# Softmax attention beside a dilated window on one core: the first sixteen score blocks under a bound from the first 512 keys

## The chip, the core and the metric

The kernel runs on one core of one Trainium2 chip. A core has five engines with queues of their own: TensorE (PE, matrix products; its weight loads are shown as PEld), VectorE (DVE), ScalarE (ACT, the exponentials), GpSimd (POOL) and SyncE (SP), which here issues nearly all transfers. Each engine works through its instructions in the order in which they were compiled, and waits where an operand is not there yet. The metric is the device time of one execution in microseconds (us); lower is better.

## The reference, cut to what matters

```python
# x: 2048 x 512; H = 32 heads of Dh = 16
def _A_ref(x, wqkv, wo):                     # full attention
    q, k, v = heads(x @ wqkv)
    scores = einsum("bhqd,bhkd->bhqk", q, k) * Dh ** -0.5
    p = softmax(scores)                      # 2048 keys for every query
    return concat(einsum("bhqk,bhkd->bhqd", p, v)) @ wo

def _B_ref(x, wqkv, wo):                     # 8 keys per query: s, s-2, ..., s-14
    q, k, v = heads(x @ wqkv)
    logits = einsum("bhsd,bhswd->bhsw", q, gather(k)) * Dh ** -0.5   # masked below 0
    return concat(einsum("bhsw,bhswd->bhsd", softmax(logits), gather(v))) @ wo

g = sigmoid((x * gate_w).sum(-1))
return g * _A_ref(x, A_wqkv, A_wo) + (1 - g) * _B_ref(x, B_wqkv, B_wo)
```

The bulk of the arithmetic is branch A: 32 heads x 2048 queries x 2048 keys exponentials.

## The kernel before, in words

**Branch A.** A *block* is one head, one tile of 128 keys and one chunk of 512 queries: a 128x512 square of transposed scores. There are 32 x 16 x 4 = 2048 blocks. Four heads form a group `i` (8 groups), and a *period* is one group with one query chunk `c_`, 64 blocks; there are 32 periods, chunks innermost. For each block TensorE multiplies a K tile (`ktg`, a strip of 32 rows per head) with Q (`qtg`), an exponential is taken, and TensorE multiplies the result `pT` into an accumulator bank with V (`vp_all`, with a 17th column that gathers the denominator). A row more in Q and K subtracts, inside the score product, a bound on the score: the sum over the head's 16 dimensions of |q| times the largest |k| of that dimension. Softmax does not depend on what is subtracted, as long as it is the same for all keys of a query.

Most exponentials are ScalarE's: the score products write into two rings in PSUM, `rA` (three blocks) and `rB` (two), and ScalarE takes one set of three or two in one instruction (`ex` in `new_set`, tiles `pT`). Some blocks go another way: "d" blocks are done by VectorE in four instructions (`p1` to `p4`, tiles `dg` and `pd`), "g" blocks by VectorE and GpSimd in one and six (`g1` to `g4`, tiles `gt`); g blocks come only when branch B is through. Their scores stand in one of three shared banks (`bank`).

**The start.** `load_x` brings x transposed in four strips of 512 rows (`xT`), `load_w0` three small pieces of the weights for the first four heads (`w`), all in SP's queue. `warm` issues 16 products on constants. Then K of the first four heads is projected strip by strip (`kp`), VectorE takes the largest |k| of each strip (`km`), ScalarE copies the strip to `ktg[0]` (`kc`); `selk_f` joins the four maxima, and `q_direct` projects Q for chunk 0, takes |q| (`absq`), multiplies it with `selk` and adds the bound to Q (`qe`). Only then can a score product be issued. `v_proj` projects V for eight key tiles at a time, in two halves. Later groups' K and Q come from `k_pack` and `q_pack`, packed for 128 columns and brought into place by transfers.

**Branch B** works on 16 tiles of 128 positions (`b_tile`): TensorE projects, the K and V rows go to memory and come back shifted for the eight neighbours (`sh`, four loads of four neighbours), and GpSimd multiplies and sums: `logits_half` twice, then softmax, then `av_half` twice. TensorE transposes the result `obb` into `obt`.

**The end.** `po1` to `po3` divide and transpose a period's accumulator into `oat`; the output projection adds `obt` times `bwo` and `oat` times `woP` and writes `out`. Three kinds (`mode`): plain, "fa" (all but the last group first, the rest added by VectorE) and "ring".

**What sets the order.** None of it is written in order. Each piece is an `Op` with engine, assumed duration, dependencies, buffers and a due time; `Scheduler.run` plays them through against these numbers, and the instructions are issued in the order that comes out. `Feeder` makes the attention blocks as it goes. The constants at the head (`CFG`, `OVER`, `HOLD`, `GSTEP`, ...) steer the choice. In places where TensorE would pause, `fill` adds products of zeros (`zeros`, shown as `ones_t,z`). All instructions are recorded in one helper, so the profile has line L299 for nearly everything; tiles tell them apart.

Of the kernel before, what the change touches and what calls it, by code (L numbers as in the profile page):

```python
# [18 lines left out]
    b_start=30.0,  # L19
    b_space=43.0,  # L20
    t0=18.0,
    t1=860.0,
    d_rem=1,
    d_min=14,
    d_end=10,
    fa2=-30.0,
# [70 lines left out]
OVER = 20.0  # L97
HOLD = 3.5
SPAN, STREAM = 3.3, 2.5
WAVE, SWITCH, JOIN = 0.222, 0.10, 0.05  # L100
GSTEP = 1.95
# [147 lines left out]
def kernel(  # L249
# [89 lines left out]
    periods = [(c_, i) for i in range(NG) for c_ in range(NC)]  # L339
# [22 lines left out]
    selk = const.tile([128, 128], BF16, name="selk")  # L362
    mask32 = const.tile([128, 32], BF16, name="mask32")
# [11 lines left out]

    def init_dve():
        V.memset(ones_t[:], 1.0)
# [10 lines left out]
        V.memset(z32[:], 0.0)  # L388
        V.memset(gw[:], 0.0)

# [3 lines left out]
    def init_pool2():  # L394
        G.memset(vp_all[:, 0, :, :], VS)
        G.memset(vp_all[:, 1:NT, 0:8, DH:DH + 1], VS)
# [21 lines left out]
    o_init_d = op("dve", 2.5, init_dve, -9.0)  # L418
    o_cr = [op("dve", 1.6, const_rows((1,), (0,)), -8.0, deps=[o_init_d])]
    o_cr.append(op("dve", 0.8, const_rows((), (1,)), 24.0, deps=[o_init_d], rel=20.0))  # L420
    o_cr += [op("dve", 1.6, const_rows((b,), (b,)), 70.0 + 20 * b, deps=[o_init_d], rel=60.0) for b in (2, 3)]
    o_id = op("pool", 1.2, init_pool, -9.0)
    o_init_p = op("pool", 1.5, init_pool2, -8.0, deps=[o_id])
    o_init_p3 = op("pool", 6.0, init_pool3, -7.0, deps=[o_init_p])

# [32 lines left out]
    o_x = [op("sp", 0.5, load_x(0), -9.0, lat=5.0)]  # L458
    o_w0k = op("sp", 0.5, load_w0(1), -8.9, lat=6.0, alloc=[tw0])
    o_x.append(op("sp", 0.5, load_x(1), -8.8, lat=6.5))  # L460
    o_w0q = op("sp", 0.5, load_w0(0), -8.75, lat=7.0, use=[tw0])
    o_x.append(op("sp", 0.5, load_x(2), -8.7, lat=8.0))
    o_x.append(op("sp", 0.5, load_x(3), -8.6, lat=9.5))
    o_w0v = op("sp", 0.5, load_w0(2), -8.55, lat=9.5, use=[tw0])
# [5 lines left out]

    def warm():
# [4 lines left out]
    o_warm = op("pe", 2.0, warm, -9.0, deps=[o_init_d], alloc=[wtok])  # L476

    o_xt = [[o] for o in o_x]

    kt_tok = {i: tok(f"kt{i % 4}", 1) for i in range(NG)}  # L480
# [9 lines left out]
    for sc in range(NC):  # L490
        st = {}
        tk = bank()

        def kp(sc=sc, st=st, tk=tk):
            st["p"] = bank_tile(tk)
            for c in range(DC):
                mm_w0(st["p"], c, 1, xT[:, c, sc * QW:(sc + 1) * QW], c == 0, c == DC - 1)
# [7 lines left out]
        a = op("pe", 0.9, kp, -2.0 + sc, deps=[o_w0k] + o_xt[sc], alloc=[tk], use=[tw0])  # L505
        km0_ops.append(op("dve", 0.7, km, -1.0 + sc, deps=[a, o_init_d], use=[tk]))
        o_kr[0, sc] = op("act", 0.65, kc, -1.0 + sc, deps=[a, o_init_d], use=[tk, kt_tok[0]] if sc else [tk],
                         alloc=[] if sc else [kt_tok[0]])
# [5 lines left out]

    def q_direct(c_, dl):
# [3 lines left out]
        def qp():  # L519
            st["p"] = bank_tile(tk_q)  # L520
            for c in range(DC):
                mm_w0(st["p"], c, 0, xT[:, c, c_ * QW:(c_ + 1) * QW], c == 0, c == DC - 1)

        def qc():
            V.tensor_scalar(out=qtg[0][:, c_, :], in0=st["p"][:], scalar1=rowc[:, 2:3], scalar2=rowc[:, 3:4],
                            op0=ALU.mult, op1=ALU.add)
            st["a"] = work.tile([128, QW], BF16, name="absq", tag="absq", bufs=1)
            V.tensor_scalar(out=st["a"][:].bitcast(U16), in0=qtg[0][:, c_, :].bitcast(U16), scalar1=32767,
# [6 lines left out]
        def qe():  # L535
            V.tensor_tensor(out=qtg[0][:, c_, :], in0=qtg[0][:, c_, :], in1=st["b"][:], op=ALU.add)
        a = op("pe", 0.9, qp, dl, deps=[o_w0q] + o_xt[c_], alloc=[tk_q], use=[tw0])
        a = op("dve", 1.1, qc, dl + 0.9, deps=[a] + o_cr[:1], use=[tk_q] + ([qt_tok[0]] if c_ else []),
               alloc=[ta_q] + ([] if c_ else [qt_tok[0]]))
        a = op("pe", 0.25, qb, dl + 2.8, deps=[a, o_selk], alloc=[tk_b], use=[ta_q])  # L540
        o_qr[0, c_] = [op("dve", 0.7, qe, dl + 3.0, deps=[a], use=[tk_b, qt_tok[0]])]

    NDQ = 2
    for c_ in range(NDQ):
        q_direct(c_, -0.5 if c_ == 0 else 24.0)
# [3 lines left out]
    def k_pack(cc):  # L549
# [3 lines left out]
        for sc in range(NC):  # L553
            dl = base - 95.0 + 9.0 * sc if cc else 40.0 + 1.5 * sc
# [40 lines left out]
        o = op("sp", 0.6 * 4 * len(gs), sct, dl + 10 if cc else 48.0, deps=evs + (o_cr if cc else o_cr[:1]),  # L595
# [5 lines left out]
    def q_pack(cc):  # L601
# [5 lines left out]
        for c in range(NC):  # L607
            dl = base - 48.0 + 6.0 * c if cc else 46.0 + 1.5 * c
# [39 lines left out]
        def sct():  # L648
            for g in range(2):
                c0 = 0 if cc or g else NDQ  # L650
                qt = qtg[(2 * cc + g) % 4]
# [709 lines left out]
```

## Time and profile before

| | |
|---|---|
| median of three runs | 870.23 us (869.83 to 870.89) |
| the profiled execution's own time | 873.02 us |
| its span, first to last instruction | 871.1 us |
| ScalarE busy | 842.1 us, 97% |
| TensorE busy | 793.5 us, 91% |
| VectorE busy | 756.2 us, 87% |
| GpSimd busy | 713.5 us, 82% |
| 16 DMA engines, share by the largest queue | 19.5% |
| blocks on ScalarE, VectorE, GpSimd | 1818, 216, 14 |

Busy time counts an engine once where its instructions overlap, so the mean of one instruction times the count is more than the busy time. "a <- b" behind an idle time names what ended it. The timeline's columns are start, duration, engine, line, operation, out<-in, shape and count. Of a wait the profile names the releaser that came last.

### The profile page before, as it was taken

What the parts mean: (1) busy time and instruction counts of PE and PEld (TensorE: products, weight loads), DVE (VectorE), ACT (ScalarE), POOL (GpSimd) and SP (SyncE); (2) the same over time, 40 slices, a digit from 0 to 9 for tenths busy, and PEclk for the clock granted to TensorE, in tenths of its full rate; (3) what the DMA queues carried; (4) which work ended last, traced back from release to release, by engine and by line L of the source; (5) the groups of instructions that cost most, each with busy time, mean ns of one, the idle gap of its engine ahead of it and who ended that gap; (6) DMA issues with size and microseconds to landing.
All of it is one profiled execution on the core that took longest, in us unless ns stands there. A gap on an engine that the chain in (4) does not pass through costs nothing.

```text
span 871.1 us, 18136 instructions
## 1 busy us (share of the span) xinstructions
PE 793.5 (91%) x7076; PEld 253.5 (29%) x7076; DVE 756.2 (87%) x1228; ACT 842.1 (97%) x751; POOL 713.5 (82%) x737
## 2 busy tenths in 40 slices
PE   6998999998899998999989999998989888899997
PEld 3223333232223332222222333222222222222232
DVE  5989898989999889998999898989889999887665
ACT  2999999999999999999999999999999999999996
POOL 2268989989997999799969997999699964886772
PEclk9999999999999999999999999999999999999999
DMA  9513202223111112221202020401321000000001
GB/s 235 178 19 119 69 26 71 51 55 130 49 61 50 61 50 60 75 78 59 86 26 85 25 86 26 109 26 38 108 76 49 25 2 1 1 2 8 20 26 49
DMA packets 54781, 51.55 MB, mean 59 GB/s; under 512 B 13628, under 2 KB 51172, under 8 KB 54696
## 3 DMA queue, kind: packets, MB, share of 16 engines
q1 hardware_dynamic: 54408, 50.14, 19.5%
q8 instruction: 55, 0.90, 0.4%
q14 instruction: 30, 0.25, 0.1%
q10 hardware_dynamic: 288, 0.26, 0.1%
HBM read 38.04 MB, written 6.33 MB: 51 GB/s over the span
## 4 chain that ended last, share of the span: by engine, by line
ACT 59%; issue 19%; PE 12%; POOL 7%; DVE 1%; SPq 1%; DMA 1%; ACTq 0%; POOLq 0%; DVEq 0%
ACT pT L299 58%; PE bank L299 8%; POOL prod L299 5%; PE ring L299 4%; SPq L299 1%; DMA w<-in_A_wqkv_dram 1%; ACT lg L299 1%; DVE dg L299 0%; POOL lg L299 0%; DMA sh<-kv_scr 0%; POOL ob L299 0%; POOL obb L299 0%; POOL ott L299 0%; DVE accT L299 0%; DVE pd L299 0%
## 5 line engine op out<-in xcount | busy, mean ns | idle before, releaser
L299 ACT ACTIVATE pT<-ring 128x1536 bf16<-128x1536 f32 x727 | 834.1, 1271 | 9.8 <-PE ring L299 6.6
L299 PE MATMUL ring<-qt,kt 32*128 32x512 bf16 x1818 | 290.2, 384 | 53.1 <-ACT pT L299 50.5
L299 DVE SCALAR_TENSOR_TENSOR dg<-bank,dg 128x512 bf16<-128x512 uint16 x432 | 297.1, 688 | 13.3
L299 PE MATMUL bank<-pT,vp_all 128*17 128x512 bf16 (+1 forms) x1818 | 290.6, 384 | 12.8 <-ACT pT L299 9.9
L299 POOL TENSOR_TENSOR prod<-prod 128x512 f32<-128x512 f32 (+1 forms) x208 | 240.4, 1169 | 6.3
L299 DVE TENSOR_SCALAR dg<-bank 128x512 bf16<-128x512 uint16 x216 | 146.8, 679 | 37.2 <-PE bank L299 29.4
L299 PEld LDWEIGHTS <-kt 32*128 32x128 bf16 x2048 | 88.8, 91 | 290.1 <-issue 286.8
L299 POOL TENSOR_TENSOR prod<-sh,qb 128x512 f32<-128x512 bf16 x128 | 143.7, 1154 | 33.7 <-DVE pd L299 32.6
L299 DVE TENSOR_TENSOR pd<-bank,dg 128x512 uint16<-128x512 f32 x216 | 148.9, 689 | 7.6 <-PE bank L299 0.3
L299 PEld LDWEIGHTS <-vp_all 128*17 128x17 bf16 (+1 forms) x2048 | 92.4, 88 | 215.9 <-issue 194.4
L299 PE MATMUL bank<-ones_t,z 128*32 128x512 bf16 x458 | 148.7, 384 | 0.0
L299 POOL TENSOR_TENSOR prod<-sh,lg 128x512 f32<-128x512 bf16 x128 | 137.5, 1106 | 2.1
L299 PE MATMUL bank<-qt,kt 32*128 32x512 bf16 x230 | 88.1, 386 | 0.2
L299 PE MATMUL bank<-pd,vp_all 128*17 128x512 bf16 x216 | 76.9, 385 | 0.1
L299 PE MATMUL bank<-bw,xT 128*32 128x512 bf16 x768 | 68.5, 383 | 0.0
L299 POOL TENSOR_SCALAR gt<-gt 128x512 f32<-128x512 uint16 (+2 forms) x42 | 38.1, 908 | 20.9 <-DVE gt L299 17.9
L299 POOL TENSOR_TENSOR gt<-gt 128x512 f32<-128x512 f32 x42 | 50.0, 1191 | 3.4
L299 PEld LDWEIGHTS <-z 128*32 128x32 bf16 x458 | 37.2, 95 | 40.9 <-issue 27.1
L299 PE MATMUL bank<-xT,wst 128*32 128x512 bf16 x512 | 44.9, 383 | 0.0
L299 PEld LDWEIGHTS <-xT 128*32 128x32 bf16 (+1 forms) x1088 | 32.6, 97 | 26.4 <-issue 19.4
L299 POOL TENSOR_TENSOR rr<-rr,omg 128x32 f32<-128x32 f32 x16 | 3.8, 238 | 33.8 <-DVE rr L299 25.9
L299 DVE STREAM_TRANSPOSE accT<-bank 128x512 f32<-128x512 f32 x32 | 22.7, 709 | 6.1 <-PE bank L299 6.0
(87 smaller groups left out, 418.6 us busy)
## 6 DMA issues: line engine op xcount, KB each, us to landing
sh<-kv_scr SPq DMA_DIRECT2D x64, 512.0 KB
kv_scr<-kvs SPq DMA_DIRECT2D x16, 256.0 KB
kt<-kpk SPq DMA_DIRECT2D x28, 64.0 KB
qt<-qpk SPq DMA_DIRECT2D x28, 64.0 KB
out_dram<-osb SPq DMA_DIRECT2D x14, 128.0 KB
wst<-in_A_wqkv_dram SPq DMA_DIRECT2D x3, 512.0 KB
bw<-in_B_wqkv_dram SPq DMA_DIRECT2D x1, 1536.0 KB
bwo<-in_B_wo_dram SPq DMA_DIRECT2D x1, 512.0 KB
```

What stands on the lines that cost most here:

```text
L299: return chain_on(key, f(*a, **k))
```

## The change

The first 16 blocks (group 0, chunk 0, key tiles 0 to 3, four heads) are bounded by the maximum of the first key strip alone. Their Q is kept apart without a bound (`qf`); a second product of `kneg` (minus the strip's maxima) with `absq` subtracts the bound inside the score product's bank. Their products with V go to an accumulator of their own (`acc_tok["f"]`). When the other strips are there, the two bounds' difference gives a factor per head and query: `rs` forms it with two products (`selb`, `sele`), ScalarE takes the exponential of half of it (`rf`), and VectorE multiplies the accumulator with it twice (`rx`); `po1` adds it to period 0's accumulator, which begins with key tile 4.

Around it: two pieces of the first weights are issued by ScalarE, not SP; the products that stood on `selq` at the start are 13 products of zeros issued at once, and `fill` may add such while they run; K strips 1 and 2 are copied by VectorE; the projections of K, of Q (chunk 1) and of V are cut into smaller pieces; Q's transfers are issued head group by head group; GpSimd handles two neighbours in one instruction; the last eight periods run with the two last groups side by side for each chunk, so the output projection of chunk 2 is plain too; due times and assumed durations differ.

In the compiled order ScalarE has 363 sets of three, 364 of two and 2 of one (364, 363 and none before), VectorE 211 blocks, GpSimd 18. Products of zeros go from 458 to 431, those at the start included. GpSimd has 192 instructions fewer in branch B.

```diff
 CFG = dict(
-    b_start=30.0,
-    b_space=43.0,
-    t0=18.0,
-    t1=860.0,
+    b_start=28.0,
+    b_space=40.0,
+    t0=9.0,
+    t1=848.0,
...
-OVER = 20.0
-HOLD = 3.5
+OVER = 15.0
+HOLD = 1.5
+DQ_DL = 0.6
...
-GSTEP = 1.95
+GSTEP = 2.1
...
-    periods = [(c_, i) for i in range(NG) for c_ in range(NC)]
+    periods = ([(c_, i) for i in range(NG - 2) for c_ in range(NC)] +
+               [(c_, i) for c_ in range(NC) for i in (NG - 2, NG - 1)])
...
-                SP.dma_start(out=w0[:, :, part, :], in_=a_w3[:, :, part * D:part * D + 80])
+                (SP if part == 2 else A).dma_start(out=w0[:, :, part, :], in_=a_w3[:, :, part * D:part * D + 80])
...
+    def zero_w():
+        mm(st_w["t"][0:32, :], z32[:], ones_t[:], True, True, tile_position=(0, 0))
+
     def warm():
-        t_ = bank_tile(wtok)
-        for _ in range(4):
-            mm_ct(t_, selq[:], ones_t[:], True, True)
+        st_w["t"] = bank_tile(wtok)
+        for _ in range(WARM):
+            zero_w()
...
         def kc(sc=sc, st=st):
-            A.activation(out=ktg[0][:, sc * QW:(sc + 1) * QW], in_=st["p"][:], func=ACT.Identity,
-                         scale=rowc[:, 0:1], bias=rowc[:, 1:2])
+            dst = ktg[0][:, sc * QW:(sc + 1) * QW]
+            if sc in KACT:
+                A.activation(out=dst, in_=st["p"][:], func=ACT.Identity, scale=rowc[:, 0:1], bias=rowc[:, 1:2])
+            else:
+                V.tensor_scalar(out=dst, in0=st["p"][:], scalar1=rowc[:, 0:1], scalar2=rowc[:, 1:2], op0=ALU.mult, op1=ALU.add)
...
+    def kneg_f():
+        V.tensor_scalar(out=kneg[:], in0=ones_t[:, 0:128], scalar1=km0[:, 0:1], scalar2=-1.0, op0=ALU.mult, op1=ALU.mult)
+
+    def selb_f():
+        V.tensor_scalar(out=selb[:], in0=selb[:], scalar1=km0[:, 0:1], scalar2=None, op0=ALU.mult)
...
+        def rs():
+            st["s"] = bank_tile(tk_s)
+            mm_ct(st["s"], selb[:], st["a"][:], True, False)
+            mm_ct(st["s"], sele[:], qtg[0][:, 0, :], False, True)
+
+        def rf():
+            st["f"] = work.tile([128, QW], FP32, name="accT", tag="accT", bufs=2)[:]
+            A.activation(out=st["f"], in_=st["s"][:], func=ACT.Exp, scale=0.5 * LN2 / BITS)
+
+        def rx():
+            st["h"] = work.tile([128, QW], FP32, name="accT", tag="accT", bufs=2)[:]
+            V.tensor_tensor(out=st["h"], in0=acc_tiles["f"][:], in1=st["f"], op=ALU.mult)
+            V.tensor_tensor(out=st["h"], in0=st["h"], in1=st["f"], op=ALU.mult)
...
-    for tb in (0, 8):
-        v_proj(0, 4, tb, 8, 3.0 + tb * 0.2, 0.0, lambda c: w0[:, c, 2, 0:64], o_w0v, (tw0,))
+    for tb, n in ((0, 4), (4, 4), (8, 8)):
+        v_proj(0, 4, tb, n, (4.0 + tb) if tb else VP0, (0.0, VA, VB)[tb // 4], lambda c: w0[:, c, 2, 0:64], o_w0v, (tw0,), n)
...
-                for w_ in range(WH):
-                    G.tensor_tensor(out=prod[:, w_, :], in0=ksh[:, w_, :], in1=qb[:], op=ALU.mult)
+                for w_ in range(0, WH, GW):
+                    G.tensor_tensor(out=prod[:, w_:w_ + GW, :], in0=ksh[:, w_:w_ + GW, :],
+                                    in1=_ap(qb[:], [list(qb[:].ap[0]), [0, GW], [1, D]]), op=ALU.mult)
...
-                    ws = min(WH, max(1, D // (H * n)))
+                    ws = min(WH, max(1, GW * D // (H * n)))
...
-                n = WH
-                while n > 2:
-                    n //= 2
-                    for w_ in range(n):
-                        G.tensor_tensor(out=prod[:, w_, :], in0=prod[:, w_, :], in1=prod[:, n + w_, :], op=ALU.add)
+                G.tensor_tensor(out=prod[:, 0:2, :], in0=prod[:, 0:2, :], in1=prod[:, 2:4, :], op=ALU.add)
...
-        l0 = op("pool", 9.5, logits_half(0), tb + 8, deps=[ld[0], qa], alloc=[tlg], use=[tsh[0], tqb], name=f"lg{t}")
-        l1 = op("pool", 9.6, logits_half(1), tb + 18, deps=[l0, ld[1]], use=[tsh[1], tqb, tlg])
+        l0 = op("pool", 8.95, logits_half(0), tb + 8, deps=[ld[0], qa], alloc=[tlg], use=[tsh[0], tqb], name=f"lg{t}")
+        l1 = op("pool", 9.05, logits_half(1), tb + 18, deps=[l0, ld[1]], use=[tsh[1], tqb, tlg])
...
-        a0 = op("pool", 9.3, av_half(0), tb + 40, deps=[a, ld[2], o_g], alloc=[tob], use=[tlg, tsh[2], trr], name=f"av{t}")
-        a1 = op("pool", 9.6, av_half(1), tb + 48, deps=[a0, ld[3]], alloc=[tbb], use=[tlg, tsh[3], tob])
+        a0 = op("pool", 8.8, av_half(0), tb + 40, deps=[a, ld[2], o_g], alloc=[tob], use=[tlg, tsh[2], trr], name=f"av{t}")
+        a1 = op("pool", 9.1, av_half(1), tb + 48, deps=[a0, ld[3]], alloc=[tbb], use=[tlg, tsh[3], tob])
...
     def zeros():
-        for pi in sorted(acc_tiles, reverse=True):
+        if st_w:
+            zero_w()
+            return
+        for pi in sorted((x for x in acc_tiles if x != "f"), reverse=True):
...
+                if fold:
+                    for s_, (pi, t, j) in enumerate(us):
+                        mm(st["r"][:, s_, :], kneg[32 * j:32 * j + DH, :], st_f["st"]["a"][32 * j:32 * j + DH, :], False, True,
+                           tile_position=(32 * j, 0))
...
-            V.transpose(out=st["a"][:].rearrange("p b d -> p (b d)"), in_=acc_tiles[pi][:])
+            src = acc_tiles[pi][:]
+            if pi == 0:
+                src = st_f["st"]["h"]
+                V.tensor_tensor(out=src, in0=src, in1=acc_tiles[0][:], op=ALU.add)
+            V.transpose(out=st["a"][:].rearrange("p b d -> p (b d)"), in_=src)
```

More of the change, by code (lines that the diff above doesn't have):

```diff
@@ L374, with init_z @@
     omg = const.tile([128, NT], FP32, name="omg")
+    def init_z():
+        V.memset(z32[:], 0.0)
+        V.memset(ones_t[:], 1.0)
     def init_dve():
-        V.memset(ones_t[:], 1.0)
         V.memset(selq[:], 0.0)
@@ L395, in init_pool2 @@
         G.memset(vp_all[:, 0, :, :], VS)
+        G.memset(vp_all[:, TPC, 4, :], VS)
         G.memset(vp_all[:, 1:NT, 0:8, DH:DH + 1], VS)
@@ new lines, in q_direct @@
+        fold = c_ == 0
+        tqf = [tok("bnd", 1)] if fold else []
+        n = DC if fold else 1
+        a = op("pe", 0.265 * n, qp(0, n), dl, deps=[o_w0q] + o_xt[c_], alloc=[tk_q], use=[tw0])
+        for c in range(n, DC, n):
+            a = op("pe", 0.265 * n, qp(c, n), dl, after=[a], use=[tk_q, tw0])
+        a = op("dve", 1.1, qc, dl + 0.9, deps=[a] + o_cr[:1], use=[tk_q] + ([] if fold else [qt_tok[0]]),
+               alloc=[ta_q] + tqf)
+        if fold:
+            st_f["st"], st_f["qc"] = st, a
+            ta_q.ops.append(o_fold)
+            tqf[0].ops.append(o_fold)
+            dl = FOLD0
@@ L685, in s @@
                     st["pv"] = bank_tile(tk, (128, TB, n))
-                for tt in range(half * TB // 2, (half + 1) * TB // 2):
+                for tt in range(half * TB // P, (half + 1) * TB // P):
                     t = tb + tt
@@ L762 @@
     WH = W // 2
+    GW = 2
     def b_tile(t):
@@ L917 @@
         b_tile(t)
-    acc_tok = {pi: bank() for pi in range(NP)}
-    acc_tiles = {}
-    todo = {(pi, j): NT for pi in range(NP) for j in range(4)}
+    T1ST = [0 if pi else TPC for pi in range(NP)]
+    todo = {(pi, j): NT - T1ST[pi] for pi in range(NP) for j in range(4)}
     o_end = {pi: op(None, 0.0, lambda: None, 0.0, deps=[], name=f"end{pi}",
```

249 lines of the change are left out of this document (170 added, 79 removed).

## The prediction

> **What bounds the kernel now.** I read the page's first part, then the exponentials as one stretch, then the groups with shapes kept apart. The windows' columns are length, then busy time with count for PE, PEld, DVE, ACT and POOL, granted PE clock, DMA share, GB/s.
>
> ```profile
> PE 793.5 (91%) x7076; PEld 253.5 (29%) x7076; DVE 756.2 (87%) x1228; ACT 842.1 (97%) x751; POOL 713.5 (82%) x737
> ```
> ```profile
> 20.47:862.79 842.32, 776.05 (x6850) 245.27 (x6849) 742.13 (x1175) 836.50 (x744) 709.06 (x723) 1.00 0.18 55
> 100.00:700.00 600.00, 551.39 (x4683) 173.47 (x4682) 543.36 (x865) 596.88 (x534) 545.08 (x558) 0.99 0.21 62
> ```
> ```profile
> L299 ACT ACTIVATE pT<-ring 128x1536 bf16<-128x1536 f32 x364 | 539.2, 1481 | 7.4 <-PE ring L299 6.6 <-PE bank L299 0.2
> L299 ACT ACTIVATE pT<-ring 128x1024 bf16<-128x1024 f32 x363 | 384.6, 1060 | 2.5 <-PE bank L299 2.1
> ```
>
> ScalarE is the bound. From its first exponential (20.47 us) to the end of its last (862.79) it works 836.50 of 842.32 us: 5.8 us of idle. So the span is start, plus ScalarE's work, plus its idle, plus an end of 871.1 - 862.79 = 8.3 us. Work taken from VectorE, GpSimd or TensorE alone buys nothing here. An earlier first exponential, less work in ScalarE's queue or less idle there does.
>
> The start, in order of time (start, duration, engine):
>
> ```profile
> 0.79 1.45 SPq L299 DMA_TRANSPOSE xT<-in_A_x_dram  x1
> 0.96 0.48 DVE L299 MEMSET ones_t<- 128x512 bf16 x1 [0.96 <-PEq L1345]
> 2.30 1.28 SPq L299 DMA_DIRECT2D w<-in_A_wqkv_dram  x1
> 3.62 2.49 SPq L299 DMA_TRANSPOSE xT<-in_A_x_dram  x1
> 6.27 0.14 PEld L299 LDWEIGHTS <-w 128*32 128x32 bf16 x8 [2.80 <-DMA w<-in_A_wqkv_dram]
> 6.79 4.13 SPq L299 DMA_TRANSPOSE xT<-in_A_x_dram  x2
> 7.53 0.15 PEld L299 LDWEIGHTS <-w 128*32 128x32 bf16 x1 [0.27 <-issue]
> 8.22 0.69 DVE L299 TENSOR_REDUCE km<-bank 128x1 f32<-128x512 f32 x1 [2.61 <-PE bank L299]
> 8.95 0.78 ACT L299 ACTIVATE kt<-bank,rowc 128x512 bf16<-128x512 f32 x1 [6.89 <-DVE km L299]
> 9.48 1.72 PEld L299 LDWEIGHTS <-w 128*32 128x32 bf16 x32 [0.25 <-DMA w<-in_A_wqkv_dram]
> 10.89 0.81 DVE L299 TENSOR_SCALAR qt<-bank,rowc 128x512 bf16<-128x512 f32 x1 [0.17 <-PE bank L299]
> 10.96 0.58 SPq L299 DMA_DIRECT2D w<-in_A_wqkv_dram  x1
> 11.73 0.29 DVE L299 TENSOR_SCALAR absq<-qt 128x512 uint16<-128x512 uint16 x1
> 13.84 0.55 PEld L299 LDWEIGHTS <-w 128*32 128x32 bf16 x16 [1.61 <-DMA xT<-in_A_x_dram]
> 15.86 0.25 DVE L299 TENSOR_SCALAR selk<-selq,km 128x128 bf16<-128x128 bf16 x1
> 16.42 1.70 PEld L299 LDWEIGHTS <-xT 128*128 128x128 bf16 x32 [2.03 <-DMA w<-in_A_wqkv_dram]
> 18.39 0.69 DVE L299 TENSOR_SCALAR vp_all<-bank 128x512 bf16<-128x512 f32 x1 [2.28 <-PE bank L299]
> 20.03 0.39 PE L299 MATMUL ring<-qt,kt 32*128 32x512 bf16 x3
> 20.47 13.73 ACT L299 ACTIVATE pT<-ring 128x1536 bf16<-128x1536 f32 x12 [4.03 <-PE ring L299]
> ```
> ```profile
> 16.50:17.00 0.50, 0.50 (x12) 0.50 (x13) 0.00 (x0) 0.00 (x0) 0.00 (x0) 0.50 1.08 377
> ```
>
> Three waits stack up. The bound on the scores needs the maximum over all four key strips, so the first score product stands behind the last transpose of x (13.84). Behind that, TensorE's order holds 32 V products whose weights land at 16.42. And TensorE is slow: four waves of the first projection start 0.42 us apart (6.27 to 7.53), later eight take 1.72 us (0.215 each), and after the gap before 16.42 the granted clock is 0.50.
>
> **The change part by part.** Positions of instructions come from the compiled order of both kernels, durations from the rows.
>
> *First exponential.* The 16 blocks of head group 0, query chunk 0, key tiles 0 to 3 need strip 0 only. TensorE gets 14 zero products from 1.45 (the `ones_t` memset), then 40 projection products, then the first set's score and `kneg` products. At the slow spacing zeros end at 1.45 + 14 x 0.42 = 7.3. The trace's slow phase from 6.27 to 9.48 lasted 3.2 us, so I take eight slow zeros and six fast (estimate): 1.45 + 3.4 + 1.3 = 6.1. The first two weight pieces go out on ScalarE's queue, ahead of its table load, no later than SP's first issue; the first x transpose was there by 6.27. So the first projection starts at 6.27 as before, but its last wave at 6.27 + 3 x 0.215 = 6.92. The maximum followed the last wave by 8.22 - 7.53 = 0.69: 7.61. On VectorE then: maximum 0.69, `kneg` 0.25 (as selk), qf 0.81, absq 0.29 with 0.05 between: 9.7. The K copy (ScalarE, 0.78) lies beside. Score product to exponential was 0.44: first exponential at 10.15. Gain 10.3 us. Bounds: 9.3 (maximum at 7.3, overlaps closer) and 12.4 (slow clock, below).
>
> *Inside the 16 blocks.* ScalarE does them as sets of 3, 2, 3, 2, then the K copy of strip 3 in its queue, then 3, 2, 1. Six sets of 3 and 2 pairs took 13.73 us, 2.29 a pair; set of 3 less set of 2 is 1.481 - 1.060 = 0.42, so 1.355, 0.934 and, extrapolated, 0.51 for one. Four sets end at 10.15 + 4.6 = 14.7. The K copy waits for VectorE's maximum of strip 3, behind which every later set of the fold is queued. SP issues x, x, w, x, x: the last transpose goes out 1.4 us earlier (one 1.28 issue and its gap fewer, the 0.58 one kept between), landing near 12.4. VectorE after absq at 9.7: 0.25 + 0.69 + 0.35 (half a V part) + 0.81 + 0.69 + 0.81 + 0.69 = 4.3, at best 14.0; K1 on TensorE holds it about 1.2 longer: 15.2. Wait 0.5 (0 to 2). The rescaled Q needs 1.9 more (0.25 selk, 0.69 V part, sum 0.7), while the copy and three sets give ScalarE 0.78 + 2.8: hidden; with that cover gone it costs its excess one to one.
>
> *ScalarE's extra work.* 363 sets of three, 364 of two and 2 of one instead of 364 and 363: 0.934 - 1.355 + 1.02 = +0.6. The rescale's exponential on 128x512: +0.5. One K copy now behind the first exponential: +0.8. Together 1.9. Two K copies go to VectorE and were ahead of the first exponential anyway: 0.
>
> *V products in parts.* In the order before, the V weights of heads 4 to 7 stand as 8 products, three others, then 24 ahead of the next score product:
>
> ```profile
> 75.77 1.27 PE L299 MATMUL bank<-wst,xT 128*128 128x128 bf16 x24
> 77.49 2.37 ACT L299 ACTIVATE pT<-ring 128x1024 bf16<-128x1024 f32 x2 [2.09 <-PE bank L299]
> ```
>
> This is the longest idle of the stretch. In the new order they stand as 16 and 16 apart, with score products between: -2.1 (0 if the wait comes back elsewhere). In the fold the first V part is 16 products in two pieces; its weights leave SP near 4.8 and took 16.42 - 10.96 = 5.5 then: 10.3, when set 2 has been issued. No cost.
>
> *GpSimd.* Per tile of branch B 12 instructions disappear into neighbours of double size, 192 in all.
>
> ```profile
> 653.16 4.49 POOL L299 TENSOR_TENSOR prod<-sh,qb 128x512 f32<-128x512 bf16 x4
> L299 POOL TENSOR_TENSOR prod<-prod 128x512 f32<-128x512 f32 x176 | 220.8, 1270 | 3.8
> L299 POOL TENSOR_TENSOR prod<-prod 128x256 f32<-128x256 f32 x32 | 19.6, 613 | 2.5
> 662.55 0.22 POOL L299 TENSOR_TENSOR rden<-rden,gall 128x16 f32<-128x16 f32 x1
> L299 POOL TENSOR_TENSOR gt<-gt 128x512 f32<-128x512 f32 x42 | 50.0, 1191 | 3.4
> ```
>
> 256 to 512 elements doubles the time (no fixed part, saving 0); 16 elements cost 0.22, a fixed part near 0.19. I take 0.1 between them: 192 x 0.1 = 19 us, about what four more GpSimd blocks (18 for 14, six instructions each) take. GpSimd idles 55 of 600 us between 100 and 700: effect on the time 0, so long as that cover lasts.
>
> *The rest.*
>
> ```profile
> L299 DVE SCALAR_TENSOR_TENSOR dg<-bank,dg 128x512 bf16<-128x512 uint16 x432 | 297.1, 688 | 13.3
> ```
>
> VectorE does 211 blocks for 216 (four such instructions each, 5 x 2.75 us less) and some 5 us of new start work: 0. The qt transfers by head group pass no one that ScalarE waits for: 0. The new order of the last eight periods moves chunk 0 to 2's output ahead; behind the last exponential stands the same chain, 8.3 us (one block instead of three: 0; 0.5 either way).
>
> ```profile
> 863.27 0.72 DVE L299 STREAM_TRANSPOSE accT<-bank 128x512 f32<-128x512 f32 x1 [3.06 <-PE bank L299]
> 867.99 0.34 ACTq L299 DMA_DIRECT2D out_dram<-osb  x1
> ```
>
> *Sum.* -10.3 + 0.5 + 1.9 - 2.1 = -10.0 us. Span 871.1 becomes 861.1, and the profiled execution's 873.02 becomes 863.0. The median of the runs shown is 870.23, 0.3% under that execution: 860.2.
>
> **The rivals.** *TensorE slow at the start.* If all fourteen zeros and the projections run at 0.42, the first projection starts at 7.3, its maximum is 1.7 later than above, and the fold's other products (some 30 waves of 0.2) cost double while ScalarE has about 8 us of work: up to 3 us more. 860.2 + 1.7 + 2 = 864. For it: two slow phases in the trace. Against: 3 us of zeros first. The Trainium skill's TensorE: Matmul & The Clock Gate, section "What's actually happening", calls the window of about 3.4 us free-running and the number of slow products variable between runs; by that rule either case can come, and I give this one a sixth.
>
> *New waits in the new order.* Every instruction is re-timed. A dip of the clock cost 0.5 us of ScalarE in one such stretch:
>
> ```profile
> 610.00:612.00 2.00, 2.00 (x14) 0.32 (x12) 1.64 (x3) 1.51 (x2) 2.00 (x3) 0.50 0.79 221
> ```
>
> and about 1 us in its whole; fill products fall from 458 to 431, warm-up included. Two dips and one wait like that of 2.09: +4, 864.
>
> *GpSimd late (the other side).* The order counts on halves of 8.95 to 9.1 us instead of 9.3 to 9.6, 2.1 a tile. The old halves measured 662.55 - 653.16 = 9.4. With no saving each tile is late by about 1.5 us, 24 by the last, and TensorE's transposes of `obb` stand in its queue ahead of score products. If half is absorbed in idle, +12: 872, slower. It decides once lateness passes 10 us, 0.6 a tile, a saving under 0.07 per dropped instruction. The 613 and 1270 rows speak for it, the 55 idle us against. The Trainium skill's GPSIMD Engine Reference, section 3.1, gives 4497 ns for 2048 fp32 elements; by that rate 512 would take 1.12, which leaves 0.15 of the 1.270 row but nothing of the 4.49 / 4 row, so an estimate by the page is a saving of 0 to 0.15.
>
> *No effect.* The earlier start is lost again because a later stage sets the pace: 870. Only 5.8 us idle in 842 speaks against it.
>
> **How the numbers follow.** Forecast as summed (857.5 to 862.5): 0.50. Slow start: 0.16. New waits: 0.14. GpSimd late: 0.13. No effect within 0.2%, about what a measurement here can tell from none: 0.04. Better than 857.5 (the remaining 3.7 us of idle shrinks too): 0.03. Faster 0.83, same 0.04, slower 0.13. The range runs to 857.0 (idle gone on top) and 868.5 (both slow start and waits).
>
> **What would show it.** First exponential at 10 us (not 12); waves of the first projection 0.215 apart; ScalarE idle before the second K copy under 2 us; ScalarE busy about 838 between first and last exponential, idle 4 to 5; no wait of 2 us near the V products of heads 4 to 7; a merged GpSimd instruction under 2.2 us. Wrong if TensorE waits for `obb` or gt tiles, or the exponentials start later than 13.

## The result, and the profile after

After ran at a median of 865.84 us (864.65 to 866.90, four executions) beside 870.56 for before: ratio 0.9946, 95% interval 0.9929 to 0.9963. Two later runs of both kernels, side by side, gave 0.9928 (0.9902 to 0.9954) and 0.9926 (0.9900 to 0.9952). All 22 executions of after have their median at 866.25, and the 122 of before that ran beside the later experiments at 872.03. So the change is worth 4.7 us in the first run and some 6 us over all, where the prediction said 10.0: 860.2, from 857.0 to 868.5.

The next lines are all of after: the first part of the page, the stretch from the first exponential to the end of the last, and ScalarE's groups. In a window line the length comes first, then busy time with count for PE, PEld, DVE, ACT and POOL, then the granted clock, the DMA share and GB/s.

```profile
PE 790.7 (92%) x7057; PEld 252.6 (29%) x7057; DVE 747.6 (87%) x1230; ACT 842.2 (98%) x752; POOL 712.9 (83%) x570
```
```profile
10.52:855.64 845.12, 778.32 (x6930) 246.03 (x6929) 736.72 (x1169) 839.10 (x748) 708.61 (x555) 0.99 0.20 58
```
```profile
L313 ACT ACTIVATE pT<-ring 128x1536 bf16<-128x1536 f32 x363 | 540.2, 1488 | 5.6 <-PE ring L313 3.9 <-PE bank L313 0.7
L313 ACT ACTIVATE pT<-ring 128x1024 bf16<-128x1024 f32 x364 | 388.0, 1066 | 0.5
L313 ACT ACTIVATE pT<-ring 128x512 bf16<-128x512 f32 x2 | 1.2, 598 | 0.5 <-PE ring L313 0.5
L313 ACT ACTIVATE accT<-bank 128x512 f32<-128x512 f32 x1 | 0.6, 618 | 0.0
```

The first exponential came 9.95 us earlier (10.52 for 20.47), and ScalarE is still the bound. But the stretch is longer: 845.12 us for 842.32, with 839.10 busy for 836.50 and 6.0 idle for 5.8. The 2.1 us of idle that should have gone are there again, in other places. ScalarE's timeline of after shows the first five waits behind the first exponential:

```profile
8.49 0.78 ACT L313 ACTIVATE kt<-bank,rowc 128x512 bf16<-128x512 f32 x1 [5.40 <-DVE km L313]
10.52 4.73 ACT L313 ACTIVATE pT<-ring 128x1536 bf16<-128x1536 f32 x4 [1.25 <-PE ring L313]
15.95 0.78 ACT L313 ACTIVATE kt<-bank,rowc 128x512 bf16<-128x512 f32 x1 [0.69 <-DVE km L313]
16.62 2.35 ACT L313 ACTIVATE pT<-ring 128x1536 bf16<-128x1536 f32 x2
19.49 3.93 ACT L313 ACTIVATE pT<-ring 128x512 bf16<-128x512 f32 x4 [0.52 <-PE ring L313]
...
40.80 9.47 ACT L313 ACTIVATE pT<-ring 128x1536 bf16<-128x1536 f32 x8 [0.23 <-PE ring L313]
50.96 1.45 ACT L313 ACTIVATE pT<-ring 128x1536 bf16<-128x1536 f32 x1 [0.69 <-PE ring L313]
...
61.08 1.45 ACT L313 ACTIVATE pT<-ring 128x1536 bf16<-128x1536 f32 x1 [0.28 <-PE bank L313]
```

Two waits of the fold (0.69 and 0.52, together 1.2 us), then 0.23, 0.69 and 0.28 (1.2 us) between 40 and 62 us, where before had none. (The fold is the first sixteen blocks with their own bound.) TensorE's timeline says what stood ahead of the fold's last score product (18.81), of the one at 50.47 and of the one at 60.58:

```profile
18.59 0.37 PE L313 MATMUL bank<-qt,kt 32*128 32x512 bf16 x1 [0.80 <-DVE qt L313]
18.81 0.37 PE L313 MATMUL ring<-qf,kt 32*128 32x512 bf16 x1
...
49.51 0.61 PE L313 MATMUL bank<-xT,wst 128*32 128x512 bf16 x8 [0.73 <-DVE qpk L313]
49.94 0.38 PE L313 MATMUL bank<-ones_t,z 128*32 128x512 bf16 x1
49.95 0.58 PE L313 MATMUL bank<-pT,vp_all 128*17 128x512 bf16 x3
50.47 0.39 PE L313 MATMUL ring<-qt,kt 32*128 32x512 bf16 x3
...
60.03 0.40 PE L313 MATMUL bank<-absq,selp 128*32 128x512 bf16 x4 [0.36 <-DVE absq L313]
```

All three are VectorE being late: a d block's score product waits for the rescaled Q (`qe`) with the fold's last set queued behind it, a packed projection waits for a bank that VectorE has not copied out, and a product of the bound waits for `absq`. The wait of 0.23 is another kind: sixteen products of a packed projection stand ahead of it, and TensorE waits for nothing there. This is read off the trace; no run takes that VectorE work away.

### The profile page after: what moved, and what is told of

Read it like the earlier page. It is cut to its first block, busy times and chain, and to the rows that moved or that the text cites. A ratio compares the mean times of both kernels' runs of the same rounds, so it can differ in the third digit from the quotient of the medians.

```text
span 863.7 us, 17936 instructions
## 1 busy us (share of the span) xinstructions
PE 790.7 (92%) x7057; PEld 252.6 (29%) x7057; DVE 747.6 (87%) x1230; ACT 842.2 (98%) x752; POOL 712.9 (83%) x570
## 4 chain that ended last, share of the span: by engine, by line
ACT 57%; PE 21%; issue 17%; DVE 3%; DMA 0%; SPq 0%; ACTq 0%; DVEq 0%
ACT pT L313 56%; PE bank L313 15%; PE ring L313 7%; DVE dg L313 1%; ACT lg L313 1%; DVE absq L313 0%; DVE pd L313 0%; DVE accT L313 0%; DMA qt<-qpk 0%; DVE qpk L313 0%; DVE selp L313 0%; DVE kmp L313 0%; DVE kpk L313 0%; SPq L313 0%; ACT kt L313 0%
## 5 line engine op out<-in xcount | busy, mean ns | idle before, releaser
L313 DVE SCALAR_TENSOR_TENSOR dg<-bank,dg 128x512 bf16<-128x512 uint16 x422 | 290.4, 688 | 13.0
L313 POOL TENSOR_TENSOR prod<-prod 128x1024 f32<-128x1024 f32 (+1 forms) x144 | 231.3, 1606 | 11.3
L313 DVE TENSOR_SCALAR dg<-bank 128x512 bf16<-128x512 uint16 x211 | 143.2, 679 | 42.1 <-PE bank L313 36.7
L313 POOL TENSOR_TENSOR prod<-sh,qb 128x1024 f32<-128x1024 bf16 x64 | 135.0, 2131 | 38.0 <-DMA sh<-kv_scr 37.2
L313 DVE TENSOR_TENSOR pd<-bank,dg 128x512 uint16<-128x512 f32 x211 | 145.3, 689 | 6.8
L313 PE MATMUL bank<-ones_t,z 128*32 128x512 bf16 x431 | 143.2, 394 | 1.5 <-DVE ones_t L313 1.5
L313 POOL TENSOR_TENSOR prod<-sh,lg 128x1024 f32<-128x1024 bf16 x64 | 127.5, 2013 | 2.4
L313 POOL TENSOR_TENSOR gt<-gt 128x512 f32<-128x512 f32 x54 | 64.4, 1192 | 4.4
L313 POOL TENSOR_SCALAR gt<-gt 128x512 f32<-128x512 uint16 (+2 forms) x54 | 49.0, 908 | 12.9 <-DVE gt L313 8.9
```

The lines of the kernel that those rows point to most:

```text
L313: return chain_on(key, f(*a, **k))
```

## The experiments

Each was run beside before on one chip; medians in us.

| run | median | lowest to highest, n | ratio to before, 95% |
|---|---|---|---|
| e1 before again | 871.76 | 870.14 to 876.65, 12 | 0.9994 (0.9972 to 1.0016) |
| e2 no fold | 871.26 | 865.36 to 873.25, 12 | 0.9987 (0.9970 to 1.0005) |
| e3 one neighbour | 869.19 | 864.75 to 874.91, 12 | 0.9959 (0.9937 to 0.9981) |
| e4 before, Q by head group | 868.97 | 867.85 to 872.22, 12 | 0.9964 (0.9947 to 0.9981) |
| f1 after again | 866.41 | 864.46 to 870.26, 9 | 0.9928 (0.9902 to 0.9954) |
| f2 zeros ahead of strip 3 | 867.34 | 864.60 to 868.83, 9 | 0.9928 (0.9903 to 0.9953) |
| f3 strip 3 assumed late | 868.10 | 865.45 to 872.49, 12 | 0.9946 (0.9924 to 0.9968) |
| f4 no fold, zeros | 869.80 | 866.20 to 875.07, 12 | 0.9963 (0.9937 to 0.9990) |
| g1 more zeros | 875.97 | 874.24 to 882.98, 9 | 1.0064 (1.0038 to 1.0090) |
| g2 Q together | 870.35 | 865.70 to 873.95, 12 | 0.9978 (0.9956 to 0.9999) |
| g3 before, more zeros | 879.32 | 877.21 to 881.88, 6 | 1.0086 (1.0064 to 1.0108) |
| g4 no zeros at the start | 866.62 | 865.47 to 868.04, 6 | 0.9939 (0.9917 to 0.9960) |
| h1 fewer zeros | 867.76 | 865.85 to 876.45, 12 | 0.9963 (0.9937 to 0.9989) |
| h2 old period order | 872.50 | 865.53 to 874.94, 12 | 0.9985 (0.9960 to 1.0011) |
| h3 after, third time | 866.10 | 863.92 to 869.16, 9 | 0.9926 (0.9900 to 0.9952) |

**e1: how typical was before's profile?** No edit.

> The kernel before, unchanged, for a second profiled execution. The first took 873.02 us, 2.5 above the 870.56 of its runs. Theory A (that excess belonged to one execution, so the 0.3% by which the prediction was scaled from execution to median was no property of the kernel): time 870.5, span near 868.7, and the 2.5 us are missing at the start or in TensorE's clock; the wait of 2.1 us near 77 us is there again, since it is made by the order. Rival B (the wait of 2.1 us is what that execution had and others have not): span 868.7, no wait over 0.6 us between 70 and 80 us. Rival C (a profiled execution of this kernel is always that much slower): span 871 and the same waits.

None of the three as written. The profiled execution took 876.65, so the excess was not one execution's: before scatters from 869.2 to 881.0, and the three executions ahead of the prediction lay at its low end. Rival B is out: the wait of 2.1 us is there in both profiles. The first exponential at 20.47 is not: it came at 19.19. Rows of ScalarE's timeline:

```profile
19.19 36.07 ACT L299 ACTIVATE pT<-ring 128x1536 bf16<-128x1536 f32 x31 [1.67 <-PE ring L299]
...
76.42 4.62 ACT L299 ACTIVATE pT<-ring 128x1024 bf16<-128x1024 f32 x4 [2.10 <-PE bank L299]
```

**e4 and g2: which part took the 2.1 us wait away?** e4 makes this edit in before, g2 undoes it in after:

```diff
-        def sct():
-            for g in range(2):
+        def sct(g):
...
-        o = op("sp", 4.8, sct, dl + 1.0, ..., lat=7.3)
-        o2 = op("sp", 4.8, scb, dl + 3.0, ..., lat=7.3)
+        for g in range(2):
+            o = op("sp", 2.4, sct(g), dl + 1.0 + 5.0 * g, ..., lat=4.9)
+            o2 = op("sp", 0.6 * nb, scb(g), dl + 3.0 + 5.0 * g, ..., lat=0.6 * nb + 2.5)
```

> Before, with one edit: the transfers of Q are issued head group by head group, as in after. Theory A (the wait of 2.1 us near 77 us came from fourteen transfers of Q for two head groups, after which the order allowed the first set of chunk 2; the V products only stood in the hole): the wait goes, 868.4 (867.5 to 869.5), first exponential still at 20.5. Rival B (as the prediction had it: the wait comes from V products standing together, and goes only when they are cut): wait of 2 us still there, 870.5.

> After with one part undone: the transfers of Q go out for two head groups together, as before. Theory A (this part took the wait of 2.1 us away): a wait of ScalarE of 1 to 2 us comes back at the beginning of chunk 2, near 68 us, behind 32 V products that stand together in the order; median 866.4 + 1.5 = 867.9 (867 to 869.5). Rival B (the V products in parts took it away): no such wait, median 866.4 within 0.7.

Theory A in both, as far as the wait goes. With Q's transfers for two head groups in one piece the planner lets the first set of chunk 2 start only after all fourteen, and fills the hole with V products; by head group there is no hole. e4's median lies in Theory A's range, though its first exponential came at 18.14 and not at 20.5; g2's is 0.85 us above it. e4's ScalarE, from its first exponential to its end, and its timeline around the old place (no wait):

```profile
18.14:858.17 840.03, 774.39 (x6837) 246.68 (x6836) 732.32 (x1160) 837.08 (x746) 709.08 (x723) 1.00 0.19 56
```
```profile
66.41 45.59 ACT L299 ACTIVATE pT<-ring 128x1024 bf16<-128x1024 f32 x40
```

2.95 us of idle for 5.8. In g2 the hole is back, at 74 us and not at 68 (PE, then ACT):

```profile
71.37 1.07 PE L313 MATMUL bank<-wst,xT 128*128 128x128 bf16 x16
72.50 0.39 PE L313 MATMUL bank<-pT,vp_all 128*17 128x512 bf16 x3
72.82 0.64 PE L313 MATMUL bank<-wst,xT 128*128 128x64 bf16 x16
```
```profile
74.23 3.28 ACT L313 ACTIVATE pT<-ring 128x1024 bf16<-128x1024 f32 x3 [1.13 <-PE bank L313]
```

This part alone takes before to 0.9964, and its undoing takes after from 0.9927 to 0.9978. The hole in g2 is only 1.1 of the 4 us that its median lost: its profile also has 2.5 us of idle in phases at 0.50, two of them (79 to 86 and 318 to 325 us) with nearly all of it.

**e2 and f4: what is the fold worth?** e2 leaves the fold out of after; f4 adds ten products of zeros ahead of strip 3's K projection (the second part of the diff):

```diff
-        fold = c_ == 0
+        fold = False
...
-            self.nfold = 4 * TPC
+            self.nfold = 0
...
-    T1ST = [0 if pi else TPC for pi in range(NP)]
+    T1ST = [0 for pi in range(NP)]
```
```diff
                     st["p"] = bank_tile(tk)
+                    if sc == 3:
+                        for _ in range(10):
+                            mm(st["p"][0:32, :], z32[:], ones_t[:], True, True, tile_position=(0, 0))
```

> After without the first sixteen blocks' own bound: all blocks wait for the maximum over four strips; the earlier weights, zero products, smaller V parts, Q transfers by head group, GpSimd steps and period order stay. Theory A (the fold carries the gain): first exponential near 17.5 us instead of 10.5 (+7.0), less the fold's own costs on ScalarE: exponential of the rescale 0.5, one K copy 0.8, two sets more 0.6, waits 1.2, together -3.1; so 865.8 + 3.9 = 869.7 (868.5 to 871). Rival B (the earlier start is lost again later, the gain comes from the rest): 866, within 1 us of after.

> After without the fold, as in the second run, and with ten products of zeros ahead of strip 3's K projection. It measures what the fold is worth when TensorE's clock does not fall. Theory A (the fold's worth is its earlier start less its costs: 7.0 - 3.1 = 3.9 us, and the 871.3 of the second run was that plus a slow start): first exponential near 17.5 us, granted clock 1.00 to 33 us, 867.5 to 869. Rival B (a fold costs more than that, as the one execution of 865.4 without it says): 865 to 866.

Theory A's direction, but both medians lie above its ranges, by 0.3 and 0.8 us: the fold is worth 3.4 us (f4) to 5 (e2). The first exponentials came at 20.04 (e2) and 18.99 (f4), not near 17.5. TensorE's rows of e2, then of f4, show the wait for the last strip of x without and with zeros ahead of it; in e2 the clock is 0.50 from 17 to 33 us, in f4 it stays at 1.00:

```profile
15.51 1.08 PE L313 MATMUL bank<-xT,w 128*32 128x512 bf16 x16 [2.45 <-DMA xT<-in_A_x_dram]
```
```profile
12.30 2.32 PE L313 MATMUL bank<-ones_t,z 128*32 128x512 bf16 x10
15.04 1.05 PE L313 MATMUL bank<-xT,w 128*32 128x512 bf16 x16 [0.41 <-DMA xT<-in_A_x_dram]
```

The fold saves some 8 us at the start. The stretch of f4 says where the rest goes:

```profile
18.99:860.23 841.24, 777.52 (x6847) 244.18 (x6846) 738.73 (x1173) 835.16 (x743) 709.15 (x555) 0.99 0.19 56
```

First exponential 8.5 us later than after's 10.52, but ScalarE busy 835.16 for 839.10. Those 3.9 us are the fold's: four more blocks fall to ScalarE (1819 for 1815, 4 x 0.42 = 1.7), the rescale's exponential (0.6), a K copy behind the first exponential (0.8), two short sets and less overlap. ScalarE's idle is 6.0 us in after's profile and 6.1 in f4's, but f4's holds some 3 us from two phases at 0.50 and after's 1.4 to 1.9; outside such phases after idles some 1.2 us more. So some 5 of 8.5 us go back, which fits the 3.4 of the medians.

**e3: the GpSimd steps.** After with one neighbour per step and before's assumed durations (`GW = 1`; 9.5, 9.6, 9.3, 9.6).

> After with one neighbour per GpSimd step and the assumed GpSimd durations of before. Theory A (GpSimd is not waited for, and a merged instruction saved only 0.1 to 0.2 us): 865.8 with 1 us either way from the re-timed order; ScalarE idle 6 to 7 us. Rival B (the merged steps give back GpSimd time that the kernel needs): 868 or more, with ScalarE's idle grown by 2 us. Rival C (the tighter planned GpSimd times are what made the new small waits): 864.5 or less.

The median is Rival B's, but not for its reason. The twelve executions lie in two groups: five from 864.8 to 867.1, with after's median (866.26), and seven from 868.6 to 874.9. The profiled one (871.0) is of the second, and its loss comes before any GpSimd step of branch B. TensorE, ScalarE, and windows of 3.4 us with TensorE's columns alone (length, busy with count, clock, DMA, GB/s):

```profile
15.66 1.90 PE L313 MATMUL bank<-xT,w 128*32 128x512 bf16 x16 [1.85 <-DMA xT<-in_A_x_dram]
17.49 0.62 PE L313 MATMUL ring<-qf,kt 32*128 32x512 bf16 x4
```
```profile
18.33 0.78 ACT L313 ACTIVATE kt<-bank,rowc 128x512 bf16<-128x512 f32 x1 [3.46 <-DVE km L313]
20.03 2.52 ACT L313 ACTIVATE pT<-ring 128x1536 bf16<-128x1536 f32 x2 [0.92 <-PE bank L313]
24.60 0.60 ACT L313 ACTIVATE pT<-ring 128x512 bf16<-128x512 f32 x1 [2.05 <-PE ring L313]
```
```profile
12.90:16.30 3.40, 1.55 (x20) 0.83 0.96 265
16.30:19.70 3.40, 3.40 (x25) 0.50 0.90 278
19.70:23.10 3.40, 2.61 (x31) 0.50 1.02 411
23.10:26.50 3.40, 3.40 (x14) 0.50 1.07 281
26.50:29.90 3.40, 3.30 (x23) 0.50 0.18 46
29.90:33.30 3.40, 3.40 (x48) 0.66 0.02 5
```

The last strip of x landed at 15.6 (in after's profile before 14.1), TensorE stood for 1.85 us, and the clock stayed at 0.50 for 17 us: ScalarE idles 7.9 us between 15 and 34 us, for 1.3 in after. The profiles of h2 and g1, below, have the same wait, 1.86 and 1.87 us, with 17 and 6.8 us at 0.50 behind it. Three waits that agree to 0.02 us do not look like a landing that merely scatters; what fixes them is open. The merged steps themselves measure 2131, 2013 and 2344 ns for two, 0.1 to 0.2 us saved each, and no TensorE wait for `obb` shows in the traces of before and after.

**f1 and h3: does after's start fall into that, too?** No edit.

> After, unchanged. Theory A (whether the last strip of x lands before TensorE has used up its other work decides the start: if not, TensorE stands idle for about 2 us, its clock falls to 0.50 from 15 to 32 us, and ScalarE loses 5 to 8 us): the executions lie in two groups, near 865 and near 870, as the twelve with one neighbour per GpSimd step did (864.8 to 874.9), so the median comes out above the 865.8 of the first four. Rival B (the slow start was made by one neighbour per GpSimd step): all executions between 864.6 and 867.

> After, unchanged, as the yardstick for the two runs beside it: 866.4 (865.5 to 867.5); first exponential 10.2 to 11.3 us.

Probably, but seldom: 3 of after's 22 executions were above 869, with mean granted clocks of 0.986 to 0.988. No profile of those three was kept. The three that were kept have a good start, with first exponentials at 10.52, 11.01 (f1) and 10.80 (h3):

```profile
11.01 4.73 ACT L313 ACTIVATE pT<-ring 128x1536 bf16<-128x1536 f32 x4 [1.25 <-PE ring L313]
```
```profile
10.80 4.73 ACT L313 ACTIVATE pT<-ring 128x1536 bf16<-128x1536 f32 x4 [1.25 <-PE ring L313]
```

If the slower executions of e3 and h2 are those that wait for x, as their one profile each does, more than half of theirs wait, with the same instructions at the start. Why is not settled.

**f2 and f3: can the start be made safe?** f2 puts eight products of zeros ahead of strip 3's K projection (as in f4). f3 changes one assumption:

```diff
-    o_x += [..., op("sp", 2.1, load_x(3), -8.6, lat=6.8)]
+    o_x += [..., op("sp", 2.1, load_x(3), -8.6, lat=7.9)]
```

> After with one edit: eight products of zeros (8 x 0.22 = 1.7 us) in TensorE's order ahead of the K projection of strip 3, where it stood idle for 1.85 us for the last strip of x. Theory A (the clock falls because TensorE stands idle there): granted clock 1.00 from 10 to 33 us, no execution above 869, highest less than 3 us over the lowest; strip 3's K copy up to 1.7 us later where x is in time, so the median is 866 to 867. Rival B (zero products do not hold the clock, or it falls for another reason): 0.50 near 15 to 32 us in some executions, two groups 5 us apart as before.

> After with one number changed: the assumed time to landing of the last strip of x, 7.9 for 6.8, so that the order has set 5 of the fold and three V products ahead of strip 3's K projection, and the first VectorE block later. Theory A: a late strip no longer stops TensorE or ScalarE; idle of ScalarE between 10.5 and 20 us under 0.6 us (1.2 in after's profile, 6 in the slow one), granted clock 1.00 at the start, median 864.5 (863.5 to 866). Rival B (the start is slow for another reason): median over 867 with two groups.

f2 is Theory A in part: clock 1.00 up to 437 us in its profile and no execution above 868.83, but 4.2 us between lowest and highest where under 3 was forecast. With 3 of 22 slow in after, nine executions without one prove little, and strip 3 was there when the zeros ended, so its profile does not show them covering a late strip; f4's does. The price shows: 2.42 us of wait at the K copy for 0.69, and a median above the forecast 866 to 867. f3's start is good (no wait at the K copy, clock 1.00), but its other order waits 4.0 us between 50 and 59, around a phase at 0.50, and the median is 1.9 us above after's: Rival B's figure, for neither reason. No version beat after.

**g1, g3 and h1: the clock and the products of zeros.** One number, in after to 2.9 (737 zeros for 431) and 2.3 (311), in before to 2.9 (789 for 474, with the sixteen products on `selq` at the start, which the 458 of the section on the change leaves out):

```diff
-SPAN, STREAM = 3.3, 2.5
+SPAN, STREAM = 3.3, 2.9
```

> After with STREAM 2.9 for 2.5: the order may fill more of TensorE's pauses with products of zeros, 737 instead of 431; ScalarE's order is the same. Theory A (the new small waits are mostly clock dips: 1.6 and 2.4 us of ScalarE's idle stood in phases at 0.50 in two profiles of after): mean granted clock 0.997 or more, idle of ScalarE from first to last exponential down from 6.0 to 6.8 to about 4.5 us, median 864.5 (863.5 to 865.5). Rival B (some 65 us more of TensorE work delays score products): idle 7 us or more, median 866.5 or more.

> Before with STREAM 2.9 for 2.5 (789 products of zeros instead of 474). Two readings. The start's order is that of before: Theory A (20.47 us for the first exponential was a slow execution's; the usual one has TensorE at full clock and 18.1 to 19.2 as the two later profiles of that start) says 18.0 to 19.3; Rival B says 20 to 20.5. The stream: by Theory A the dips go as in after, 872.2 becomes 870 (869 to 871) with the 2.1 us wait still there; by Rival B the zeros delay score products and nothing is gained.

> After with STREAM 2.3 for 2.5: 311 products of zeros instead of 431. More zeros cost 10 us for 306 (0.03 us each). Theory A (the zeros themselves hold up score products, in after too): 120 fewer save up to 4 us of small waits, and more phases at 0.50 cost 0.7 us each; median 865 (863 to 866.5), mean granted clock 0.985 to 0.99. Rival B (the zeros that are left out were the ones that hold the clock): five or more new slow phases, 868 to 871.

More zeros are Rival B, far beyond it: 9.7 us for 306 products, 0.03 each, although four of the nine executions had a mean clock of 1.000 (874.2 to 874.6). The g1 profile, of the slowest execution (882.98, clock 0.989), has TensorE busy for 834.85 of 862.79 us, nearly as long as ScalarE:

```profile
10.42:873.21 862.79, 834.85 (x7234) 262.06 (x7233) 737.78 (x1169) 844.41 (x748) 709.45 (x555) 0.99 0.19 57
```

Fewer zeros are worse, too (between A and B): 867.76, with ten phases at 0.50 in its profile. So after's number of zeros is the best of the three tried, and neither more nor fewer buys off the phases that are left. g3's other reading is Theory A's: the starts of g3 and e4 have before's order, and their first exponentials come at 18.69 and 18.14. g3's:

```profile
18.69 36.53 ACT L299 ACTIVATE pT<-ring 128x1536 bf16<-128x1536 f32 x31 [1.68 <-PE ring L299]
```

**g4: the thirteen zeros at the start.** After with `WARM = 0` and no fill before strip 1.

> After without the thirteen products of zeros at the start. Theory A (they hold TensorE at full speed when the first weights land): the first projection's waves are 0.42 us apart instead of 0.22, the first exponential comes at 12 to 12.8 us instead of 10.5 to 11, and 867.5 to 868.5. Rival B (the first projection waits for its weights anyway and the slow spacing is over in a microsecond): first exponential at 11 to 11.5, 866.4 to 867.

Rival B's times, with the spacing of Theory A. The waves are 0.44 apart (forty products in 4.54 us), so the slow spacing is not over in a microsecond; but the first exponential comes at 11.47, 0.5 to 0.95 later, and the median (866.62) is not told apart from after's.

**h2: the period order.** After with the last eight periods in the old order, all due times kept.

> After with one part undone: the last eight periods in the old order (chunks innermost). Theory A (the new period order is worth its shorter end alone, 8.3 to 8.1 us): median within 0.7 of after on the same chip. Rival B (the new order of periods is what gives back part of the gain): 1 us or more below after.

Neither: it is 6.4 us slower than after beside it. Its profiled start fell into the slow clock as e3's did, and its end is long: the last exponential ends at 861.81 of a span of 872.4, 10.6 us for after's 8.1. Under the new due times the new order is worth 2.5 us at the end of that profile.

## Why the prediction was wrong

The direction and the way were right, the size was not: 10.0 us forecast, 4.7 measured in the first run and some 6 over all. The steps that failed are the first exponential, credited with 10.3 us and worth 8.3, and VectorE's part, put at nothing and measured at 1.5. The time of 865.84 lies in the stated range because the range was wide.

The executions, sorted by their mean granted clock, show that the smaller gain is no matter of luck in the draw:

| mean granted clock | before: n, median | after: n, median |
|---|---|---|
| 0.995 and more | 60, 870.99 | 3, 864.46 |
| 0.990 to 0.995 | 32, 872.53 | 16, 866.25 |
| under 0.990 | 30, 875.42 | 3, 870.09 |

5 to 6.5 us at each clock, not 10, though two of the rows have only three executions of after. Step by step, means of after's three profiles against before's two (for the start, the four that share before's: before, e1, e4, g3; for the waits from 40 to 62 us the two of after without a clock phase there):

| step | forecast | measured |
|---|---|---|
| first exponential | -10.3 | -8.3 (19.1 to 10.8) |
| waits of the fold | +0.5 | +1.2 |
| ScalarE's extra work | +1.9 | +1.9 (837.1 to 839.0) |
| wait near heads 4 to 7 | -2.1 | -2.1 |
| new waits, 40 to 62 us | 0 | +1.2 |
| the end | 0 | -0.25 |
| sum | -10.0 | -6.35 |

The measured sum is 0.6 us more than the medians' 5.8; that rest is not accounted for.

- **The step that failed most: the first exponential.** Its place in after was nearly right (10.15 forecast; 10.5 to 11.0). What was mis-sized is mainly where it had been. The prediction read 20.47 off one profile and listed three waits behind it as properties of the kernel. The third, "after the gap before 16.42 the granted clock is 0.50", and the weights that landed at 16.42, belonged to that execution: the same start gave 19.19, 18.69 and 18.14, and there TensorE does not wait for these weights. e1's row:

```profile
15.89 1.11 PE L299 MATMUL bank<-w,xT 128*128 128x64 bf16 x32
```

Of the missing 3.7 us, 2.0 are here: 1.35 from the start of before, 0.65 from after's. The forecast time also stood on three low executions of before, 870.23 for the 872.03 of 122, so it was low by another 1.8.
- **"The rest ... VectorE: 0" failed.** The cover was a share of busy time over the whole; at 18, 50 and 60 us VectorE is late, TensorE stands for 0.80, 0.73 and 0.36 behind it, and ScalarE for 0.5, 0.7 and 0.3. It is the second fold wait and two of the three new waits from 40 to 62 us, together 1.5 us of the 3.7; with the third, 1.7. The fold wait had been called hidden ("the rescaled Q needs 1.9 more", whose listed parts add to 1.64); it measured 0.52.
- **The 2.1 us wait: right sum, wrong cause.** "V products in parts" was credited; "the qt transfers by head group pass no one that ScalarE waits for" got nothing. e4 and g2 show that it is the transfers. At clocks of 0.995 and more e4's ten executions have a median of 868.84, 2.15 below before's: just that wait. The V products were what the planner put into the hole.
- **ScalarE's extra work** came out to the tenth, with some luck: before's two profiles are 1.1 us apart in it. **GpSimd:** 0.1 to 0.2 us per merged instruction for the 0.1 forecast, and no wait from it; the rival is out. Its busy time in the stretch is 708.6 us for 709.1, so the merged steps saved about what the four more blocks took. The sign "under 2.2 us" held for two of the three merged kinds; the additions take 2.34.
- **"TensorE slow at the start"** was the right place and the wrong trigger. The zeros did run at the slow spacing (13 in 5.09 us), but doing without them altogether delays the first exponential by only 0.5 to 0.95 us (g4). The loss comes when the last strip of x is late; its size, some 4 us between the medians of e3's two groups, is about what the prediction gave its rival. "The last transpose goes out 1.4 us earlier" was wrong as well: SP's issue of the last two ends at 10.67 for 10.92. In kernels with this start the strip was there by 14.1 to 14.7 us in some profiles and landed at 15.4 to 16.0 in others (13.8 to 14.9 before).
- **"New waits in the new order"** came half true: the waits have places, and VectorE is behind most of them; clock dips stood in before's profiles as much (1.0 and 4.6 us of ScalarE's idle) as in after's (some 1.5 to 3.5 in three). The reading "from 458 to 431, warm-up included" was wrong: 458 leaves the sixteen products at the start out, 431 has the thirteen in.

In e3's rows TensorE is busy for 3.40 of 3.40 us from 16.3 to 19.7, and the clock stays at 0.50 until 32 us. By the table in the Trainium skill's TensorE: Matmul & The Clock Gate, section "What's actually happening", the full clock comes after at least one busy window of about 3.4 us; here one was not enough, and the measurement decides. In the same rows the clock fell behind a pause of 1.85 us. The section "HAM oscillation — how this bites in real kernels" of that Trainium skill page warns of gaps above about 3.4 us; here 1.85 us were enough.

## What to carry to other kernels

A start that is pulled forward pays only what its own costs leave: the fold starts 8.5 us earlier here, and some 5 of them are handed back in added ScalarE work and in waits. Before a start time from one profile is subtracted, ask which of its waits hang on a transfer's landing or on the clock, and take those from several executions. Where a long run of filler products ends a wait, look for what the planner was filling: the cure was two transfers cut in half, not the products.

## What the runs showed of the hardware

A pause of TensorE of 1.85 us for one transfer was followed by 17 us of half clock (e3, h2; 6.8 us in g1) and cost some 4 us of the whole, in some executions of the same instructions and not in others. Ten products of zeros in that place (f4) left a pause of 0.41 us and a clock of 1.00. Over the whole kernel 306 more products of zeros brought a mean clock of 1.000 in four of nine executions and cost 9.7 us, 0.03 us each, more than the phases that they prevent. With 120 fewer, ten phases at 0.50 in one profile stood beside 13.3 us of ScalarE's idle, and the median of that kernel lost only 1.5.
